# Zero-padded 64-row score matmuls and a later cubic step in a fused attention and GEGLU kernel on one NeuronCore

## The chip, the cores and the metric

The kernel runs on one core of a Trainium2 chip (trn2). The metric is the device time of one execution in microseconds (us). Before the change the median of six runs was 1717.1 us (1713.9 to 1721.9); over all 16 runs of the rounds in which the two kernels were compared it was 1716.66 us.

Engine names in the profile: PE is TensorE's matmul, PEld its weight load, DVE is VectorE, ACT is ScalarE, POOL is GpSimd, SPq is the queue of SyncE from which this kernel issues its loads.

## The reference

A pre-LayerNorm attention block followed by a pre-LayerNorm feed-forward block with a gated GELU, in bfloat16, with S = 2048 rows, width D = 576, 32 heads of 18 columns and F = 4608:

```python
h  = x + A_ref(layernorm(x), wqkv, wo)          # x is A_x; B_x is not used
h2 = h + B_ref(layernorm(h), w_gate, w_up, w_down)
# A_ref: qkv = x @ wqkv; p = softmax(q k^T * 18**-0.5); (p v) @ wo
# B_ref: (gelu_tanh(x @ w_gate) * (x @ w_up)) @ w_down
```

## The kernel before

The queries are cut into 4 blocks of 512 rows, the heads into 8 groups of four. A *unit* is one head group in one block, so there are 32 units (0 to 31). A unit has 32 *passes*. In each pass TensorE computes scores for two heads and 128 keys (two matmuls of 512 columns), and ScalarE turns them into exponentials in one 128 x 1024 instruction. After every second pass TensorE multiplies four heads' exponentials by the values (the PV matmuls).

A head has 18 rows, and a 19th carries a bound that keeps the exponentials in range. So a score matmul has 19 active rows of the 128, placed at one of four 32-row tiles of the array:

```python
KTj = sb("KTj", [P, 2, S], BF16)          # keys of four heads at partitions 0, 32, 64, 96; two units
QTj = sb("QTj", [P, 2, QB], BF16)
a_sb = sb("a_sb", [P, 2, 512], BF16)      # copy of the attention accumulator

def emit_ST(i):                            # the scores of pass i
    ...
    for q_, c in enumerate(cc):            # two of the four heads
        fns.append(mm_fn(Sring[:, bankcol:bankcol + 512],
                         KTj[32 * c:32 * c + PS, s_, kt * P:(kt + 1) * P],        # PS = 19
                         QTj[32 * c:32 * c + PS, s_, :], True, True, tile_position=(32 * c, 0)))
```

All other work is put between the passes as *filler*. Units 0 to 2 carry the Q and K projections. Units 3 to 7 carry nearly nothing. Units 8 to 31 carry the previous block's output projection (Wo), its second LayerNorm and its feed-forward network (FFN). The last block's FFN runs alone after the last exponential; it is called the tail here. Fillers that cost TensorE time draw on a credit of 560 per pass (the scheduler's own unit, meant as ns). The FFN has 36 *f tiles* of 128 columns per block, in two halves of 18. Each half ends with five down projections.

```python
def ffn_gelu_a(f, tail=False):
    ...                                                                    # x2 = xb^2
    if tail: E("act",  lambda e: e.activation(x2, xb, ACTF.Square), ...)
    else:    E("pool", lambda e: e.tensor_tensor(x2, xb, xb, ALU.mult), ...)
    E("dve", lambda e: e.scalar_tensor_tensor(out=x2, in0=x2, scalar=GC1, in1=xb, op0=ALU.mult, op1=ALU.mult), ...)
    E("pool" if tail else "dve", lambda e: e.tensor_tensor(x2, x2, xb, ALU.add), ...)

def ffn_gelu_c(f):
    ...                                                                    # after tanh on ScalarE
    E("dve", lambda e: e.scalar_tensor_tensor(out=x2, in0=th, scalar=1.0, in1=xb, op0=ALU.add, op1=ALU.mult), ...)
    E("pool", lambda e: e.tensor_tensor(gT[:, fs, :], x2, ub, ALU.mult), ...)

# schedule_ffn, for each f tile; at(pass, cost, what)
    if fs == 0:
        ...ffn_load_wd for the first two down-projection tiles...
    if f % FCH == 0 and fc + 1 < NFC:
        ...ffn_load_chunk: gate and up weights of the next two f tiles...
    at(s0, 1100.0, gate)        # 5 matmuls, then the gate is copied out of PSUM (xb)
    at(s0 + 1, 1100.0, up)      # 5 matmuls, then half of the up part is copied out (ub)
    at(s0 + 2, 0.0, ffn_gelu_a)
    at(s0 + 7, 0.0, ffn_gelu_b) # tanh, ScalarE
    at(s0 + 8, 0.0, ffn_gelu_c)
    step[0] += 2                # so s0 advances by two passes per f tile
```

## Time and profile before

| Stage, from the first exponential of one unit to that of the next (the tail: from the end of the last exponential) | us |
|---|---|
| prologue (first LayerNorm, K and V projections) | 114.5 |
| units 0 to 2 (Q/K projections as filler) | 161.9 |
| units 3 to 7 (attention alone) | 152.6 |
| units 8, 16, 24 (Wo and second LayerNorm) | 120.1 |
| unit 9 (the first FFN starts) | 62.1 |
| the other twenty units (FFN as filler) | 902.3 |
| tail | 206.5 |

In the page of the profile, part 1 gives busy time, share of the span and instructions of each engine. In part 2 each digit is the share of one fortieth of the span in tenths; `PEclk` is the clock that TensorE was granted.

```profile
PE 1399.6 (81%) x7528; PEld 458.1 (27%) x7528; DVE 734.3 (43%) x1568; ACT 1126.0 (65%) x1293; POOL 387.6 (23%) x364
...
PEclk9778756555659898998788889696987998869998
```

No engine is full, and the clock stands at 5 to 7 tenths in 15 of the 40 slices. The stretches show where. Columns: from:to and length in us, busy us of each engine (with its instructions), granted clock, DMA share, GB/s.

```profile
114.50:276.40 161.90, 138.09 (x619) 49.11 (x619) 92.22 (x129) 92.02 (x97) 2.30 (x2) 0.74 0.02 8
276.40:429.00 152.60, 140.08 (x667) 27.96 (x667) 11.76 (x36) 150.19 (x162) 5.75 (x5) 0.51 0.04 13
...
469.00:1513.80 1044.80, 890.92 (x4992) 280.55 (x4992) 436.01 (x901) 765.39 (x844) 266.03 (x246) 0.84 0.22 58
1513.80:1720.20 206.40, 148.13 (x708) 61.60 (x708) 109.23 (x209) 62.84 (x108) 97.75 (x76) 0.89 0.32 78
...
278.40:455.80 177.40, 164.09 (x824) 37.99 (x823) 19.04 (x63) 168.72 (x180) 6.46 (x7) 0.50 0.04 14
```

In the second stretch ScalarE is busy 150.19 of 152.60 us: attention alone is bound by the exponentials, 30.5 us per unit. The units with the FFN as filler take 34.5 to 62 us instead, while ScalarE is at 73% there. The last line is the odd one: TensorE is busy 164.09 of 177.40 us, 92%, and its clock is half (0.50) throughout.

The clock records of this trace hold only 0.5 and 1.0, and the stretches of each are multiples of 3.41 us (the last one, at the end of the trace, aside); those at 0.5 add up to 686 us, 40% of the span. Being busy alone is not what decides here: a TensorE that is 92% busy stays slow.

The timeline (start in us, length, engine, line, operation; in brackets the idle time before the instruction and what ended it) shows the second loss. This is the FFN as filler, with the two copies out of PSUM left out:

```profile
914.89 0.69 DVE L724 SCALAR_TENSOR_TENSOR arena<-arena 128x512 bf16<-128x512 bf16 x1 [2.26 <-POOL arena L723]
915.61 0.42 DVE L726 TENSOR_TENSOR arena<-arena 128x512 bf16<-128x512 bf16 x1
...
917.15 0.68 DVE L742 SCALAR_TENSOR_TENSOR arena<-arena 128x512 bf16<-128x512 bf16 x1
917.91 1.15 POOL L744 TENSOR_TENSOR arena<-arena 128x512 bf16<-128x512 bf16 x1 [3.06 <-DVE arena L742]
919.02 1.04 POOL L723 TENSOR_TENSOR arena<-arena 128x512 bf16<-128x512 bf16 x1
920.10 0.69 DVE L724 SCALAR_TENSOR_TENSOR arena<-arena 128x512 bf16<-128x512 bf16 x1 [2.26 <-POOL arena L723]
```

L724 is the cubic step, L742 the (1 + tanh) step, L744 GpSimd's product and L723 its square. The cubic step of one tile is queued on VectorE right behind the square of the same tile, so VectorE waits. The square is queued on GpSimd behind the product of an earlier tile, which waits for VectorE's L742. VectorE and GpSimd take turns in a ring of 5.21 us per f tile, in which neither is full.

The view of waits (engine, tile and line that waited, what it waited for: us in total, times, longest) gives the sums:

```profile
DVE arena L724 <- POOL arena L723: 203.6, 90, 2.3
PE Sring L297 <- ACT PT L576: 84.7, 150, 7.1
PE Aacc L297 <- DVE a_sb L596: 33.2, 12, 4.3
PE G L296 <- DMA arena<-in_B_w_up_dram: 24.4, 10, 5.2
PE G L296 <- POOL arena L744: 17.3, 2, 8.7
```

The first line is the ring. The last is the tail: both halves' down projections wait 8.7 us for GpSimd's last products.

### The profile page before, as it was taken

How to read it: one execution, taken by the hardware profiler on the slowest of the kernel's cores; microseconds unless marked ns; L12 is line 12 of the kernel's file. 1: busy time of each engine (PE TensorE's matmuls, PEld its weight loads, DVE VectorE, ACT ScalarE, POOL GpSimd, SP SyncE). 2: the span in 40 equal slices, each digit the busy share in tenths (PEclk: the TensorE clock that was granted, in tenths of full speed). 3: DMA queues.
4: the chain of work that ended last, by engine and by line, in shares of the span. 5: the costliest groups of instructions: out<-in, count | busy, mean ns of one | idle time of the engine just before them, and what ended most of it. 6: DMA issues, size and time to landing. Idle time of an engine off the chain costs nothing.

```text
span 1720.2 us, 20569 instructions
## 1 busy us (share of the span) xinstructions
PE 1399.6 (81%) x7528; PEld 458.1 (27%) x7528; DVE 734.3 (43%) x1568; ACT 1126.0 (65%) x1293; POOL 387.6 (23%) x364
## 2 busy tenths in 40 slices
PE   2557899999978798878898887888997987968686
PEld 1223222111312232222322222223322322232222
DVE  6546543000435514531555135414553255156364
ACT  3123668999748676778787667677875786725151
POOL 1100000000014402330133114300342134007373
PEclk9778756555659898998788889696987998869998
DMA  3010000000032122211221132022221320123432
GB/s 103 14 40 6 10 10 10 12 17 10 10 92 65 37 58 75 65 34 55 70 69 50 40 89 65 23 56 69 64 60 41 80 70 24 35 69 108 89 86 49
DMA packets 193174, 87.23 MB, mean 51 GB/s; under 512 B 97968, under 2 KB 190064, under 8 KB 193072
## 3 DMA queue, kind: packets, MB, share of 16 engines
q1 hardware_dynamic: 193072, 85.91, 18.8%
q8 instruction: 59, 0.97, 0.2%
q14 instruction: 43, 0.35, 0.1%
HBM read 71.07 MB, written 2.36 MB: 43 GB/s over the span
## 4 chain that ended last, share of the span: by engine, by line
PE 37%; DVE 18%; POOL 14%; issue 14%; ACT 9%; SPq 4%; DMA 4%; POOLq 0%; ACTq 0%; DVEq 0%
PE G L296 21%; PE Sring L297 10%; ACT PT L576 9%; POOL arena L744 7%; PE Aacc L297 4%; POOL arena L723 4%; SPq L288 4%; DVE arena L724 3%; DVE arena L742 3%; DVE arena L322 2%; POOL arena L726 2%; DMA arena<-in_B_w_down_dram 2%; DVE arena L726 2%; PE G L309 1%; DMA arena<-in_B_w_up_dram 1%
## 5 line engine op out<-in xcount | busy, mean ns | idle before, releaser
L576 ACT ACTIVATE PT<-Sring 128x1024 bf16<-128x1024 f32 x1024 | 987.0, 1024 | 347.3 <-PE Sring L297 341.1
L297 PE MATMUL Sring<-QTj,KTj 19*128 19x512 bf16 x2048 | 457.9, 466 | 100.3 <-ACT PT L576 84.7
L296 PE MATMUL G<-hnT,arena 128*128 128x512 bf16 x1440 | 402.3, 418 | 63.6 <-DMA arena<-in_B_w_up_dram 24.4
L296 PE MATMUL G<-arena 128*128 128x512 bf16 (+3 forms) x1120 | 305.8, 426 | 34.9 <-POOL arena L744 17.3
L297 PE MATMUL Aacc<-PT,Vpj 128*32 128x512 bf16 x2048 | 247.5, 473 | 33.9 <-DVE a_sb L596 33.2
L744 POOL TENSOR_TENSOR arena<-arena 128x512 bf16<-128x512 bf16 x144 | 183.4, 1278 | 373.4 <-DVE arena L742 373.4
L297 PEld LDWEIGHTS Sring<-QTj,KTj 19*128 19x128 bf16 x2048 | 95.3, 94 | 475.4 <-ACT PT L576 268.3
L296 PEld LDWEIGHTS G<-hnT,arena 128*128 128x128 bf16 x1440 | 127.9, 104 | 273.1 <-issue 84.0
L724 DVE SCALAR_TENSOR_TENSOR arena<-arena 128x512 bf16<-128x512 bf16 x144 | 110.6, 768 | 203.6 <-POOL arena L723 203.6
L296 PEld LDWEIGHTS G<-arena 128*128 128x128 bf16 (+3 forms) x1120 | 118.8, 119 | 183.8 <-issue 85.0
L552 POOL COPY Vpj<-Vd 128x1152 bf16<-128x1152 bf16 x32 | 36.6, 1146 | 515.5 <-PE Aacc L297 502.1
L723 POOL TENSOR_TENSOR arena<-arena 128x512 bf16<-128x512 bf16 x108 | 112.2, 1039 | 130.3 <-DVE arena L322 130.3
L324 DVE TENSOR_SCALAR arena<-G 128x512 bf16<-128x512 f32 x144 | 98.7, 686 | 95.5 <-PE G L296 63.4
L742 DVE SCALAR_TENSOR_TENSOR arena<-arena 128x512 bf16<-128x512 bf16 x144 | 114.6, 804 | 0.3
L733 ACT ACTIVATE arena<-arena 128x512 bf16<-128x512 bf16 x144 | 89.8, 628 | 31.7 <-DVE arena L726 25.5
L297 PEld LDWEIGHTS Aacc<-PT,Vpj 128*32 128x32 bf16 x2048 | 54.5, 96 | 190.5 <-issue 188.4
L322 DVE CAST arena<-G 128x512 bf16<-128x512 f32 x108 | 74.0, 685 | 50.0 <-PE G L296 50.0
L596 DVE CAST a_sb<-Aacc 128x512 bf16<-128x512 f32 x32 | 22.0, 687 | 170.0 <-PE Aacc L297 170.0
L317 ACT ACTIVATE arena<-G 128x512 bf16<-128x512 f32 x36 | 21.5, 597 | 94.2 <-PE G L296 66.0
L393 POOL TENSOR_TENSOR lnt<-lnt,halfc 128x1 f32<-128x1 f32 x32 | 17.5, 548 | 245.0 <-DVE lnt L392 245.0
L771 DVE COPY arena<-G 128x512 f32<-128x512 f32 (+1 forms) x20 | 13.8, 688 | 106.7 <-PE G L296 106.7
L726 POOL TENSOR_TENSOR arena<-arena 128x512 bf16<-128x512 bf16 x36 | 42.2, 1173 | 41.0 <-DVE arena L724 41.0
(77 smaller groups left out, 558.8 us busy)
## 6 DMA issues: line engine op xcount, KB each, us to landing
arena<-in_B_w_gate_dram SPq DMA_DIRECT2D x72, 256.0 KB, 2.7
arena<-in_B_w_up_dram SPq DMA_DIRECT2D x72, 256.0 KB, 3.2
arena<-in_B_w_down_dram SPq DMA_DIRECT2D x32, 576.0 KB, 4.6
KTj<-KTd SPq DMA_DIRECT2D x128, 76.0 KB
QTj<-QTd SPq DMA_DIRECT2D x128, 19.0 KB
arena<-in_A_x_dram SPq DMA_DIRECT2D x4, 576.0 KB, 4.0
h_sb<-in_A_x_dram SPq DMA_DIRECT2D x4, 576.0 KB, 5.7
arena<-in_B_w_gate_dram SPq DMA_DIRECT2D x72, 32.0 KB, 2.7
```

Source lines behind the costliest of these rows:

```text
L288: fns = [(lambda o, i: lambda e: e.dma_start(o, i))(o, i) for (o, i) in pairs]
L296: return lambda e: e.matmul(dst, lhsT, rhs, start=start, stop=stop)
L297: return lambda e: e.matmul(dst, lhsT, rhs, start=start, stop=stop, tile_position=tile_position, skip_group_check=skip)
L322: E("dve", lambda e: e.tensor_copy(dst_ap, src_ap), reads=reads, writes=writes)
L324: E("dve", lambda e: e.tensor_scalar(dst_ap, src_ap, scale, None, ALU.mult), reads=reads, writes=writes)
L576: E("act", lambda e: e.activation(PT[:, pts, :], Sring[:, slot * 1024:(slot + 1) * 1024], ACTF.Exp, scale=SCALE), reads=[("S", slot * 2), ...
L723: E("pool", lambda e: e.tensor_tensor(x2, xb, xb, ALU.mult), reads=[("xb", k)], writes=[("x2", k)])
L724: E("dve", lambda e: e.scalar_tensor_tensor(out=x2, in0=x2, scalar=GC1, in1=xb, op0=ALU.mult, op1=ALU.mult), reads=[("x2", k), ("xb", k)], ...
L726: E("pool" if tail else "dve", lambda e: e.tensor_tensor(x2, x2, xb, ALU.add), reads=[("x2", k), ("xb", k)], writes=[("x2", k)])
L733: E("act", lambda e: e.activation(th, uu, ACTF.Tanh, scale=GC0), reads=[("x2", k)], writes=[("th", k)])
L742: E("dve", lambda e: e.scalar_tensor_tensor(out=x2, in0=th, scalar=1.0, in1=xb, op0=ALU.add, op1=ALU.mult), reads=[("th", k), ("xb", k)], ...
L744: E("pool", lambda e: e.tensor_tensor(gT[:, fs, :], x2, ub, ALU.mult), reads=[("ub", k), ("x2", k)], writes=[("gT", fs)])
```

## The change

The change has two aims: to get TensorE its full clock by making each score matmul cover 64 rows of the array, of which 45 are zeros, and to open the ring by moving the cubic step two passes later. Several smaller moves come with it. The core of the diff:

```diff
-    KTj = sb("KTj", [P, 2, S], BF16)
-    QTj = sb("QTj", [P, 2, QB], BF16)
+    KTj = sb("KTj", [P, 2, 2, S], BF16)
+    QTj = sb("QTj", [P, 2, 2, QB], BF16)
-    a_sb = sb("a_sb", [P, 2, 512], BF16)
+    a_sb = sb("a_sb", [P, 1, 512], BF16)
 ...                                                      # prologue
+        E("dve", (lambda s_: lambda e: e.memset(KTj[:, s_], 0.0))(s_), writes=[("KTj", s_)])
+        E("dve", (lambda s_: lambda e: e.memset(QTj[:, s_], 0.0))(s_), writes=[("QTj", s_)])
 ...                                                      # loads, each head's 19 rows
-            pairs.append((KTj[32 * c:32 * c + PS, s_, :], KTd[r0:r0 + PS, j, :]))
+            p0 = 64 * (c // 2)
+            pairs.append((KTj[p0:p0 + PS, s_, c % 2, :], KTd[r0:r0 + PS, j, :]))
 ...                                                      # emit_ST
-                             KTj[32 * c:32 * c + PS, s_, kt * P:(kt + 1) * P],
-                             QTj[32 * c:32 * c + PS, s_, :], True, True, tile_position=(32 * c, 0)))
+                             KTj[p0:p0 + 64, s_, c % 2, kt * P:(kt + 1) * P],
+                             QTj[p0:p0 + 64, s_, c % 2, 0:qb], True, True, tile_position=(p0, 0)))
 ...                                                      # ffn_up, tail only: up part copied out by ScalarE
-        evac(ub, bank[:, 0:512], [bkey], [("ub", k)], "dve", scale=0.5)
+                    evac(tmp[:, 1, k, 0:qb], bank[:, 0:qb], [bkey], [("ub", k)], "act" if tail else "dve", scale=0.5)
 ...                                                      # gelu: the cubic step and the add become ffn_gelu_a2
-        E("pool" if tail else "dve", lambda e: e.tensor_tensor(x2, x2, xb, ALU.add),
+        E("dve", lambda e: e.tensor_tensor(x2, x2, xb, ALU.add),
 ...                                                      # schedule_ffn
-                if fs == 0:
-                    ...ffn_load_wd...
-                if f % FCH == 0 and fc + 1 < NFC:
-                    ...ffn_load_chunk...
+                if f % FCH == 0 and fc + 1 < NFC:
+                    ...ffn_load_chunk...
+                if fs == 2:
+                    ...ffn_load_wd...
-                at(s0 + 2, 0.0, (lambda f: lambda: ffn_gelu_a(f, tail=tl))(f))
+                at(s0 + 2, 0.0, (lambda f: lambda: ffn_gelu_a(b, f, tail=tl))(f))
+                at(s0 + 4, 0.0, (lambda f: lambda: ffn_gelu_a2(b, f, tail=tl))(f))
 ...                                                      # Wo: three parts; the second PSUM bank is taken only at the third
-            add_bulk(base + 8 + 2 * qt, 1100.0, (lambda qt: lambda: block_Wo_qt_b(b, qt))(qt), tag)
+            add_bulk(base + 8 + 2 * lt, 900.0, (lambda lt: lambda: block_Wo_qt_b(b, lt))(lt), tag)
+            add_bulk(base + 8 + 2 * lt, 450.0, (lambda lt: lambda: block_Wo_qt_c(b, lt))(lt), tag)
```

Cut here: a table of block sizes (all remain 512 rows), hooks for the FFN's bank and phase that do nothing, a rewritten main loop, the queuing of all three parts of a down projection at one pass, and the many lines that follow from these.

The single `a_sb` buffer is what makes room.

## The prediction

> **What bounds the kernel now.** The table by stretches: prologue (0 to 114 us), attention with Q/K projections as fillers (to 276), attention alone (to 429), attention with three blocks' Wo, LN2 and FFN (to 1514), the last block's FFN alone (206 us). Attention alone runs at 30.1 us per unit (32 units, 8 head groups x 4 blocks) with ScalarE 100% busy on exponentials; 32 units at that pace would be 963 us, but they take 1399. Three causes show.

> 1. A ring of VectorE and GpSimd. In the timeline at 915 to 926 us the FFN repeats every 5.2 us per f tile: VectorE 2.95 us of work, then idle 2.26 us (203.6 us in the waits view) for GpSimd's product (1.15) and square (1.04), because the cubic step directly follows the square. Eight tiles per unit are 42 us, which is what the full-clock units 10 and 29 take. ScalarE needs 4 x 0.94 + 0.63 = 4.4 us per tile. The same blocking delays the copy of the attention accumulator (33 us of PE waits, up to 4.3 each) and, at each half's end, the tanh ahead of the exponentials (6.5 us stalls).
> 2. The clock: half rate for 40% of the time, in multiples of 3.41 us.[...] At 278 to 456 us TensorE is 92% busy and yet at half rate. Weighting matmuls by active rows x columns (scores 19/128, PV 1/4), a window under about 0.38 of full-rate work is followed by a slow one, in all but some 10 of 490 windows. A slow window costs 1.1 to 2 us (equal units 20 and 28: 43.0 and 39.6 us with 3 and 1).
> 3. In the tail GpSimd does 2.7 us per f tile; tiles pass every 3.3 us, and the down matmuls wait 8.7 us twice.

> **What the change does.**
> - Scores become 64-row tiles padded with zeros: same streaming time[...], weight 1/2 instead of 0.15. Applied to the old windows, slow ones fall from 24 to about 6 in units 0 to 2 and from 97 to about 45 from unit 9 on. Attention alone (0.33 to 0.38) mostly stays slow, at no cost.
> - The cubic step moves two steps later: the ring opens, toward 4.4 to 4.7 us per tile.
> - Tail: the add leaves GpSimd for VectorE, the up eviction goes to ScalarE (4 x 0.61 = 2.45 us per tile, the new bound).
> - Weight-load order, Wo split, single a_sb buffer: about nothing.
> - Added: zeroing KTj and QTj on VectorE before the first LN, estimated 4.5 us from the 1.48 us for 1710 words, critical.

> **Sum.** Prologue +4.5; units 0 to 2 -17; 3 to 7 -2; 8, 16, 24 -9; unit 9 -10; the other twenty from 45 to about 39 us: -125; tail -30. 1717 - 188 is about 1530 us; range 1470 to 1620. Faster by over 2%: 0.95; within: 0.035; slower: 0.015.

> **Right or wrong shows as:** VectorE's wait for the square under 40 us; mean clock about 0.85 to 0.9; gate/up units at 37 to 40 us; attention-alone units still 30; tail near 175 us, ScalarE its busiest elementwise engine; first LN about 4.5 us later.

> **Wrong if:** padding zeros don't count as activity (then about 1590); exponentials and fillers couple so that units stay above 41 us; weight loads bind the tail.

The terms come to -188.5 us, and 1717 - 188 is about 1530. What it says of the hardware stands beside these numbers: a pair of score matmuls takes 0.39 us at full clock and 0.61 at half in both profiled runs ("same streaming time"); 0.94 us is a unit of 30.1 us over its 32 exponentials; the "1.48 us for 1710 words" is VectorE's zeroing of 128 x 1710 words at 1.23 us of before. Estimates from the windows of before are the 0.38, the counts of slow windows that padding would leave, the 0.33 to 0.38 of attention alone, and the cost of a slow window (units 20 and 28 by themselves give (43.0 - 39.6) / 2 = 1.7 us).

## More of the kernel before

All loads go through one queue, SyncE's. That includes the copies of the next unit's keys and queries, which `jit_loads` issues at pass 8 of each unit as eight loads in a row (four of KTj, four of QTj).

## The result, and the profile after

The kernel after takes 1554.57 us, the median of 8 runs (1552.1 to 1557.0), against 1716.66 us. The ratio is 0.9055, with a 95% interval of 0.9035 to 0.9075. Ratios here are the mean time of one kernel's fast runs over that of the other's of the same rounds, so they are not quite the ratio of the medians quoted. Outputs were correct, as in all the runs below. The profiled runs span 1720.2 and 1552.7 us.

The same two parts of the page, for the kernel after:

```profile
PE 1276.3 (82%) x7528; PEld 442.7 (29%) x7528; DVE 824.9 (53%) x1572; ACT 1131.6 (73%) x1329; POOL 393.5 (25%) x328
...
PEclk9878899565689999999899999998999999969998
```

TensorE runs the same 7528 matmuls in 123 us less busy time, as the clock rose from 0.801 to 0.888 on average. Mainly the attention-alone part remains slow (0.61). The stretches of the kernel after, cut at the same units:

```profile
119.50:262.30 142.80, 115.17 (x620) 44.54 (x619) 92.04 (x129) 91.02 (x96) 2.30 (x2) 0.92 0.03 9
262.30:412.50 150.20, 128.44 (x667) 27.33 (x667) 11.67 (x36) 149.32 (x161) 5.75 (x5) 0.61 0.04 14
...
443.80:1365.00 921.20, 816.99 (x5005) 271.06 (x5004) 520.11 (x918) 758.05 (x844) 315.23 (x247) 0.94 0.25 66
1365.00:1552.70 187.70, 142.21 (x708) 64.96 (x708) 115.26 (x209) 78.28 (x144) 54.94 (x40) 0.88 0.35 86
```

The waits of the kernel after:

```profile
PE Sring L308 <- ACT PT L637: 89.6, 176, 5.7
PE G L307 <- DMA arena<-in_B_w_up_dram: 45.8, 16, 5.5
PE G L307 <- POOL arena L846: 15.5, 2, 7.7
DVE arena L824 <- ACT arena L815: 10.2, 4, 5.4
```

VectorE's 203.6 us for GpSimd's square are gone; of the cubic step's waits (now L824) 10.2 us for the tail's square on ScalarE are left. TensorE's 33.2 us of waits for the copy of the attention accumulator, which VectorE makes, are gone too (they are back, at 36.1 us, when experiment 4 closes the ring again). TensorE's waits for up weights rose from 24.4 to 45.8 us. The timeline of the FFN as filler, one f tile:

```profile
842.35 0.69 DVE L844 SCALAR_TENSOR_TENSOR arena<-arena 128x512 bf16<-128x512 bf16 x1
842.96 0.68 DVE L824 SCALAR_TENSOR_TENSOR arena<-arena 128x512 bf16<-128x512 bf16 x1
843.12 1.53 POOL L846 TENSOR_TENSOR arena<-arena 128x512 bf16<-128x512 bf16 x1 [1.66 <-DVE arena L844]
843.68 1.26 DVE L826 TENSOR_TENSOR arena<-arena 128x512 bf16<-128x512 bf16 x1
...
846.30 0.68 DVE L844 SCALAR_TENSOR_TENSOR arena<-arena 128x512 bf16<-128x512 bf16 x1
```

The period is now 3.95 us (842.35 to 846.30), no longer 5.21. The add (L826) takes 1.26 us where it took 0.42. It now runs beside GpSimd's product, L846, which is itself slower (1.53 against 1.15 us). In this trace 128 of VectorE's 144 adds run beside a product and take 1.25 or 1.26 us each; the other 16, beside no product, take 0.42. The products beside an add take 1.47 to 1.54 us. The mean of the adds went from 425 ns (108 of them; the tail's were GpSimd's then) to 1166 ns (all 144). Why the two slow each other when they run side by side, called their collision below, no run here shows. It costs VectorE time; what it costs of the total is taken up below.

Set against the prediction, stage by stage (the sum by stage of the profiled runs):

| Stage | before | after | change predicted | change measured |
|---|---|---|---|---|
| prologue | 114.5 | 119.5 | +4.5 | +5.0 |
| units 0 to 2 | 161.9 | 142.8 | -17 | -19.1 |
| units 3 to 7 | 152.6 | 150.2 | -2 | -2.4 |
| units 8, 16, 24 | 120.1 | 94.0 | -9 | -26.1 |
| unit 9 | 62.1 | 51.1 | -10 | -11.0 |
| other twenty units | 902.3 | 807.2 | -125 | -95.1 |
| tail | 206.5 | 187.8 | -30 | -18.7 |
| **total** | 1720.2 | 1552.7 | -188 | -167.5 |

So 30 us are missing in the twenty FFN units and 11 in the tail, while the Wo units gained 17 more than predicted. The experiments look for these, and for whether the two causes are really the two that were named.

### The profile page after: what moved, and what is told of

Its sections match the earlier page's. It is cut to its first block, busy times and chain, and to the rows that moved or that the text cites. A ratio compares the mean times of both kernels' runs of the same rounds, so it can differ in the third digit from the quotient of the medians.

```text
span 1552.7 us, 20513 instructions
## 1 busy us (share of the span) xinstructions
PE 1276.3 (82%) x7528; PEld 442.7 (29%) x7528; DVE 824.9 (53%) x1572; ACT 1131.6 (73%) x1329; POOL 393.5 (25%) x328
## 5 line engine op out<-in xcount | busy, mean ns | idle before, releaser
L308 PE MATMUL Sring<-QTj,KTj 64*128 64x512 bf16 x2048 | 428.7, 427 | 106.9 <-ACT PT L637 89.6
L307 PE MATMUL G<-hnT,arena 128*128 128x512 bf16 x1440 | 366.0, 394 | 46.6 <-DMA arena<-in_B_w_up_dram 45.8
L307 PE MATMUL G<-arena 128*128 128x512 bf16 (+3 forms) x1120 | 281.5, 401 | 29.8 <-POOL arena L846 15.5
L846 POOL TENSOR_TENSOR arena<-arena 128x512 bf16<-128x512 bf16 x144 | 213.8, 1485 | 305.1 <-DVE arena L844 282.0
L308 PE MATMUL Aacc<-PT,Vpj 128*32 128x512 bf16 x2048 | 225.6, 430 | 0.7 <-ACT PT L637 0.7
L308 PEld LDWEIGHTS Sring<-QTj,KTj 64*128 64x128 bf16 x2048 | 97.1, 94 | 436.6 <-ACT PT L637 257.7
L826 DVE TENSOR_TENSOR arena<-arena 128x512 bf16<-128x512 bf16 x144 | 167.8, 1166 | 5.0
L307 PEld LDWEIGHTS G<-arena 128*128 128x128 bf16 (+3 forms) x1120 | 112.6, 114 | 167.1 <-issue 62.2
L844 DVE SCALAR_TENSOR_TENSOR arena<-arena 128x512 bf16<-128x512 bf16 x144 | 118.1, 820 | 12.3 <-ACT arena L834 11.4
L342 DVE TENSOR_SCALAR arena<-G 128x512 bf16<-128x512 f32 x108 | 74.0, 685 | 62.4 <-PE G L307 62.0
L824 DVE SCALAR_TENSOR_TENSOR arena<-arena 128x512 bf16<-128x512 bf16 x144 | 98.2, 682 | 10.2 <-ACT arena L815 10.2
```

Of the source, the lines that this page charges most:

```text
L307: return lambda e: e.matmul(dst, lhsT, rhs, start=start, stop=stop)
L308: return lambda e: e.matmul(dst, lhsT, rhs, start=start, stop=stop, tile_position=tile_position, skip_group_check=skip)
L342: E("dve", lambda e: e.tensor_scalar(dst_ap, src_ap, scale, None, ALU.mult), reads=reads, writes=writes)
L826: E("dve", lambda e: e.tensor_tensor(x2, x2, xb, ALU.add), reads=[("x2", k), ("xb", k)], writes=[("x2", k)])
L846: E("pool", lambda e: e.tensor_tensor(gT[:, fs, 0:qb], x2, ub, ALU.mult), reads=[("ub", k), ("x2", k)], writes=[("gT", fs)])
```

## The experiments

Theory A: TensorE's clock depends on how much of its array is at work, zeros included, and the opened ring gives the rest; the missing 30 us are a new wait. Rival theories: B, the padding does nothing by itself (or the clock follows the speed of the pipeline, not the rows), and the later cubic step gives all; C, the reverse; D, the small moves have effects of their own, against the prediction's "about nothing".

Each part of the change was made alone or undone alone. In what follows "before" and "after" are the two kernels. The twelve runs came in three calls; the median of before in their rounds was 1720.28, 1719.26 and 1718.93 us. For the four runs of the second call (experiments 5 to 8) the record's own verdict against before is "unclear": before ran from 1694 to 1726 us there. What is read of these four is the median against that of after, and the stages; their own runs lie within 0.6% of each other.

### 1. The padding alone

Before, with the padded operands, the zeroing, and the single `a_sb` that it needs:

```diff
-    KTj = sb("KTj", [P, 2, S], BF16)            # QTj alike
+    KTj = sb("KTj", [P, 2, 2, S], BF16)
-                             KTj[32 * c:32 * c + PS, s_, ...], ... tile_position=(32 * c, 0)
+                             KTj[64 * (c // 2):64 * (c // 2) + 64, s_, c % 2, ...], ... tile_position=(64 * (c // 2), 0)
```

> The kernel before plus the padding alone (64-row score tiles, zeroed KTj and QTj, single a_sb for room). Clock theory (the throttle counts active rows, padded zeros too): prologue +5 us, units 0 to 2 about -19, units 8, 16, 24 about -26 together, unit 9 about -10, the other filled units about -50 through fewer slow windows, tail unchanged at 206; total about 1615 us, mean clock about 0.87. Rival (padding is only a layout; the clock rose because the stalls went away): 1717 to 1725 us, clock stays 0.80.

Measured: 1659.88 us, ratio 0.9655 (0.961 to 0.970), clock 0.873. Units 0 to 2 fell from 161.9 to 142.9 us, all that they gain in after. So B falls: zeros in the array raise the clock (0.801 in before). But the total fell by 60 us, not by the 105 expected: the other twenty units gained 34 of 50 us, units 8, 16 and 24 12 of 26, unit 9 4 of 10, and the prologue cost 7. In the FFN units the ring of VectorE and GpSimd still stands (its wait is 203.6 us here too), which limits what a faster TensorE can gain there. The clock of this kernel by fortieths of the span, to compare with the two above:

```profile
PEclk9768898555779899999899999998999998969898
```

### 2. The later cubic step alone

Before, with the cubic step and the add moved to `s0 + 4`:

```diff
+    def ffn_gelu_a2(f, tail=False):
 ...
+                at(s0 + 4, 0.0, (lambda f: lambda: ffn_gelu_a2(f, tail=tl))(f))
```

> The kernel before plus the later cubic step alone. Ring theory: VectorE's wait for the square falls from 204 us to under 40, the full-clock gate/up stretches go from 5.2 to about 4.4 us per f tile, total about 1650 us; units 0 to 2 stay at 162 us and 8, 16, 24 at 120 us because their clock is unchanged. Rival (the stalls are what slows the clock, padding does nothing): about 1560 us and clock near 0.88.

Measured: four runs from 1659.25 to 1689.12 us, two of which count as slow (over 1.5% above the fastest). The two fast ones give a ratio of 0.9692 (0.962 to 0.977), about 53 us. The profile fell in the slow state, so only what the ring's opening cannot blur is read from it: VectorE's wait for the square is gone, and units 0 to 2 still take 158 us and units 8, 16 and 24 still 120. Both causes count, and neither gives the whole, so C falls too.

### 3. After, with 19 rows again

Everything of the change except the padding: operands, loads and score matmuls as before; the zeroing is kept at its cost.

```diff
-                             KTj[p0:p0 + 64, s_, c % 2, kt * P:(kt + 1) * P], ... tile_position=(p0, 0)
+                             KTj[32 * c:32 * c + PS, s_, kt * P:(kt + 1) * P], ... tile_position=(32 * c, 0)
```

> The changed kernel with the scores back at 19 rows in 32-row tiles (zeroing kept, so the prologue stays at 119 us). Clock theory: units 0 to 2 back to about 161 us, 8, 16, 24 back to about 120, some 30 us more in the FFN units; about 1630 us, clock about 0.82. Rival (layout only): 1550 to 1560 us, clock 0.89.

Measured: 1617.39 us, ratio 0.9403 (0.936 to 0.945), clock 0.812. The padding is worth 63 us in after, as it was worth 60 in before. The stretch of units 0 to 2 of this kernel has the length and the clock that it had in before, to the digit:

```profile
119.00:280.90 161.90, 138.07 (x619) 49.04 (x619) 92.18 (x129) 91.98 (x97) 2.30 (x2) 0.74 0.02 8
```

### 4. After, with the cubic step at once

```diff
-                at(s0 + 4, 0.0, (lambda f: lambda: ffn_gelu_a2(b, f, tail=tl))(f))
+                at(s0 + 2, 0.0, (lambda f: lambda: ffn_gelu_a2(b, f, tail=tl))(f))
```

> The changed kernel with the cubic step back directly behind the square. Ring theory: VectorE waits for the square again by some 150 us or more, f tiles at 5.2 us in the gate/up stretches (108 x 0.9 = about +95), but the 4.4 us stalls for the up weights go away in exchange (about -40); about 1605 us. The product's slow-down of the add (1.26 us when it overlaps GpSimd) disappears: the add is 0.43 us again. Rival (VectorE is not what paces these units): within 1% of 1555 us.

Measured: 1610.89 us, ratio 0.9373 (0.934 to 0.941), clock 0.885. The clock is that of after (0.888), so the two causes are separate. The waits of this kernel show the ring back in full, and the wait for up weights small again:

```profile
DVE arena L824 <- POOL arena L817: 203.6, 90, 2.3
PE G L307 <- DMA arena<-in_B_w_up_dram: 18.1, 8, 5.4
```

The second line is the first hint at the missing 30 us: the wait for up weights is 18.1 us with the ring closed and 45.8 with it open (closed: 24.4 in before and 27.9 with the padding alone; open: 44.8 in experiment 3). The add takes 500 ns on the mean here, 1166 in after.

### 5. After, with 32 rows

The layout of experiment 3, but the matmul covers 32 rows (19 and 13 zeros):

```diff
-                             KTj[32 * c:32 * c + PS, s_, ...]
+                             KTj[32 * c:32 * c + 32, s_, ...]
```

> The changed kernel with scores in four 32-row tiles as before, but all 32 rows active (13 of them zeros). If the throttle counts active rows x columns, a score matmul weighs 32/128 = 0.25, between 0.148 (19 rows) and 0.5 (64 rows): applied to the windows of the 19-row variant, slow ones fall from 178 to about 160, so about 1590 us, clock about 0.83, and 0.25 should be the weight that sorts its windows best. If the throttle counts whole row groups, or only data that isn't zero, nothing changes against 19 rows: 1617 us, clock 0.81.

| Kernel (rows of a score matmul) | windows | 0.148 (19 rows) | 0.25 (32) | 0.5 (64) |
|---|---|---|---|---|
| before (19) | 491 | **0** | 19 | 76 |
| after with 19 rows | 459 | **1** | 21 | 69 |
| after with 32 rows | 451 | 10 | **0** | 38 |
| padding alone (64) | 471 | 41 | 26 | **1** |
| after (64) | 441 | 40 | 27 | **1** |

(These counts take a matmul to stream from 0.08 us after its recorded start, an offset that was fitted; without it the bold counts are 5, 4, 3, 3 and 3. The limit is sharp: at 0.36 the bold counts are 7 to 19, at 0.39 they are 7 to 12. Six more kernels, on which nothing was fitted, give 0 to 4 misses of 426 to 481 windows.)

In each kernel the weight that fits is the number of rows that the instruction covers, whether they hold data or zeros. The 92% busy stretch at half clock fits: with scores of 19 rows its 50 windows sum to 0.15 to 0.34, none to 0.375. Attention alone stays mostly slow even when padded (0.61; 7 of the 43 windows in that stretch of after reach 0.375). But there ScalarE is busy 149.32 of 150.20 us and TensorE 128.44, so the exponentials bind, and the slow clock costs nothing that shows: 30.04 us per unit, against 30.5 in before.

### 6. After, with the tail's engines as before

```diff
-                    evac(... "act" if tail else "dve", scale=0.5)
+                    evac(... "dve", scale=0.5)
-        E("dve", lambda e: e.tensor_tensor(x2, x2, xb, ALU.add),
+        E("pool" if tail else "dve", lambda e: e.tensor_tensor(x2, x2, xb, ALU.add),
```

> The changed kernel with the last block's add back on GpSimd and its up eviction back on VectorE. My reading: the tail goes back from 188 to about 205 us, everything before it unchanged; about 1572 us. Rival (the tail's gain comes from the later cubic step or the load order): tail about 190, 1555 us.

Measured: 1576.34 us, ratio 0.9205 (0.913 to 0.929), the tail at 208 us. Without these two moves nothing of the tail's gain is left (206.5 us in before), and it is some 20 us, not the 30 of the prediction.

### 7. After, with the down-projection weights loaded first

```diff
+                if fs == 0:
+                    ...ffn_load_wd...
                 if f % FCH == 0 and fc + 1 < NFC:
                     ...ffn_load_chunk...
-                if fs == 2:
-                    ...ffn_load_wd...
```

> The changed kernel with the two w_down loads issued at a half's first tile and ahead of the next w_gate/w_up chunk, as before. If this order is what took units 12, 20 and 28 from about 42 to 36 us and unit 9 down by some 8: about +28 us, 1582 us, with TensorE waiting for the up weights right after a half's start. If the order costs nothing (as I predicted): 1555 us, and the cause is elsewhere in the rest of the change.

Measured: 1569.35 us, ratio 0.9168 (0.909 to 0.925). This order is worth 15 us, about half of the 28 expected here, and the prediction had put it at nothing (D holds). The cost sits where a half of the FFN starts: unit 9 takes 60.7 us (51.1 in after), unit 12 42.0 (36.1). In the waits of this kernel the up weights stand at 57.9 us:

```profile
PE G L307 <- DMA arena<-in_B_w_up_dram: 57.9, 21, 6.6
```

### 8. After, with Wo in two parts and two banks

```diff
-            add_bulk(base + 8 + 2 * lt, 900.0, ...block_Wo_qt_b...)
-            add_bulk(base + 8 + 2 * lt, 450.0, ...block_Wo_qt_c...)
+            add_bulk(base + 8 + 2 * lt, 1100.0, ...block_Wo_qt_b...)   # _a takes both banks, as before
```

> The changed kernel with Wo back in two pieces that hold two of the three banks. If the split is what took units 8, 16 and 24 from 36 us each (padding alone) to 31: about +13 us there, 1567 us. If it is worth nothing (as I predicted): 1555 us.

Measured: 1561.14 us (1558.5 to 1567.0), ratio 0.9123 (0.902 to 0.923). By itself the total does not settle it, for the interval holds after's 0.9055. The stage does: units 8, 16 and 24 take 109.0 us instead of 94.0. Part of these 15 us comes back in unit 9 and in units 17 and 25, which get less left-over work. Whether it is the credit (2000 against 2250 per row tile) or the bank held early was not separated. What shows: in unit 8, which is 4.7 us longer than in after, TensorE waits 3.6 us for VectorE's adds and copies that follow the Wo matmuls, against 0.6 in after.

### 9. After, with the first down projection spread into the end of a half

At a half's end TensorE's scores waited up to 5.7 us behind ScalarE (first line of after's waits). The three parts of the first down projection were set 7, 5 and 2 passes earlier, to give TensorE work while the last tiles pass through the elementwise engines:

```diff
-                    at(s0, n_mm * 220.0, fn)
+                    at(s0 - (7, 5, 2)[ip] if m == 0 else s0, n_mm * 220.0, fn)
```

> The changed kernel with the first down tile's three parts issued between the last cubic/tanh chains of a half instead of after all of them. If the missing gain in the units with a half's end is the exponentials queued behind the last tanhs (stalls of 5.7 and 5.1 us, six of them, each followed by slow windows): stalls under 2 us, about 1530 us, units 11, 14, 19, 22, 27, 30 from 44 to about 39 us, tail unchanged at 188. If those stalls are paid for elsewhere anyway: within 1% of 1555.

Measured: 1546.42 us, ratio 0.9017 (0.896 to 0.908): 8 us, a third of the 25 expected; the units with a half's end fell from 43.8 to 42.3 us, not to 39. The long waits for the exponentials went, as the waits of this kernel show, but TensorE now waits at other places, for GpSimd's last products:

```profile
PE Sring L308 <- ACT PT L637: 63.4, 180, 0.7
PE G L307 <- POOL arena L846: 40.0, 8, 7.7
```

The stall moved rather than went away.

### 10. After, with the loads of keys and queries spread

Why did the units that carry only gate and up matmuls (10, 13, 18, 21, 26, 29) stay at 42 us, when the ring was open? The load queue of after shows eight key and query loads issued in a row, and the weights behind them. Here the second column is how long the queue was taken by the group:

```profile
811.82 2.58 SPq L299 DMA_DIRECT2D KTj<-KTd  x4
814.45 7.98 SPq L299 DMA_DIRECT2D QTj<-QTd  x4
822.53 3.48 SPq L299 DMA_DIRECT2D arena<-in_B_w_gate_dram  x2
826.37 1.85 SPq L299 DMA_DIRECT2D arena<-in_B_w_up_dram  x2
```

The keys and queries hold the queue for 10.6 us, and the next weights' issue begins only then. TensorE's timeline in the same unit of after shows the price: it idles 4.38 us for the up weights, and the five matmuls that follow take 2.10 us (1.25 us in the group before): its clock record, at 1.0 during the stall, is at 0.5 from 832.70 to 836.11 us.

```profile
832.43 2.10 PE L307 MATMUL G<-hnT,arena 128*128 128x512 bf16 x5 [4.38 <-DMA arena<-in_B_w_up_dram]
```

The experiment issues one head's keys and queries at each of passes 2, 8, 14 and 20, the same eight loads in all:

```diff
-        if p == min(8, blk(b)[4] - 1) and u + 1 < NU:
-            jit_loads(u + 1)
+        if p in (2, 8, 14, 20) and u + 1 < NU:
+            jit_loads(u + 1, heads=((p - 2) // 6,), copy=(p == 8))
```

> The changed kernel with the next unit's K and Q loads issued head by head over the unit instead of all eight at once. If the 4.4 us stalls for the up weights in units 10, 13, 18, 21, 26, 29 come from weight loads standing behind some 10 us of K and Q issue on the one load queue: these stalls go, those units fall from 42 to about 36 us, about 1520 us. If the weights are late for another reason (bandwidth, two slots only): stalls stay, 1555 us.

Measured: 1506.47 us, ratio 0.8792 (0.873 to 0.885), so 48 us faster than after, more than the 35 expected. The six units fell from 42 to 35.3 us each. Each load now holds the queue about 0.6 us:

```profile
800.38 0.64 SPq L299 DMA_DIRECT2D KTj<-KTd  x1
801.07 0.60 SPq L299 DMA_DIRECT2D QTj<-QTd  x1
...
806.82 0.96 SPq L299 DMA_DIRECT2D arena<-in_B_w_gate_dram  x2
```

And the wait for up weights in this kernel is

```profile
PE G L307 <- DMA arena<-in_B_w_up_dram: 14.8, 8, 5.4
```

So the missing time of the gate/up units was the load queue. In before the ring of 5.21 us per tile was slow enough to hide most of it. The packet records of the traces tell more of why eight loads in a row take 10.6 us and not eight times 0.6. The four key loads cost the queue no more in a row (2.58 us) than apart (4 x 0.64); the query loads behind them do (7.98 us). Meanwhile the rows of the keys, 76 packets of 4096 bytes, pass in single file: one every 0.155 us for most of the time from 813.3 to 826.8 us, and for every one of the 32 units of after such a group takes 12.5 to 13.7 us. The queries' rows follow only then. In experiment 10 one head's 19 rows take 3 to 4.3 us at a time, while the queue is already free. So the queue is held while the keys' rows drain; why, no run here shows.

### 11. After, with the cubic step one pass later still

```diff
-                at(s0 + 4, 0.0, (lambda f: lambda: ffn_gelu_a2(b, f, tail=tl))(f))
+                at(s0 + 5, 0.0, (lambda f: lambda: ffn_gelu_a2(b, f, tail=tl))(f))
```

> The changed kernel with the cubic step one more step later, so that the add tends not to run beside a GpSimd product. If the add's 1.17 us (0.43 before) is waiting for GpSimd and not a slower instruction: its mean falls to under 0.8 us with the same count and shape. If VectorE does not pace the units now: total within 1% of 1555 us all the same. If it does: 1535 us or less.

Measured: 1563.38 us over six runs, ratio 0.912 (0.907 to 0.917). The add fell to 929 ns only, and the total rose by 9 us (0.6%); scores now waited up to 6.4 us. The total stayed within the 1% expected, but the premise (an add of at most 0.8 us) was not reached. Nor did VectorE get time back: the cubic step rose from 682 to 914 ns, so the add's 34 us less stand against 33 more there, and VectorE is busy 821.5 us against 824.9. The collision moved from one step to the other. So this run says nothing about what the collision costs.

### 12. After with 9, 10 and the zeroing on GpSimd

```diff
-        E("dve", (lambda s_: lambda e: e.memset(KTj[:, s_], 0.0))(s_), writes=[("KTj", s_)])   # and QTj
+        if 1 <= t <= 4:                                          # between the first LayerNorm's row tiles
+            E("pool", (lambda s_, h_: lambda e: e.memset(KTj[:, s_, h_, :], 0.0))((t - 1) // 2, (t - 1) % 2), ...)
+        if 5 <= t <= 6:
+            E("pool", (lambda s_: lambda e: e.memset(QTj[:, s_], 0.0))(t - 5), ...)
```

> The half-end order and the split loads together, and the zeroing of KTj and QTj on GpSimd during the first LN tiles instead of on VectorE ahead of them. If the three costs are separate: prologue back to about 115 us, both kinds of stall gone, about 1555 - 25 - 35 - 5 = 1490 us. If they overlap: 1510 us or more.

Measured: 1504.51 us, ratio 0.8776 (0.871 to 0.885): the fastest of all, but only 2 us below experiment 10, with overlapping intervals, and between the 1490 us expected of separate costs and the 1510 of overlapping ones. The prologue gained nothing (119.4 us). LayerNorm did start at 13.5 us again and not at 18.9, but then its row tiles followed every 5.0 us and not every 3.9, and VectorE's instructions were long where they met GpSimd's zeroing. In the timeline of this kernel:

```profile
27.98 1.80 POOL L541 MEMSET KTj<- 128x2048 bf16 x1
28.53 1.42 DVE L418 TENSOR_SCALAR arena<-arena,lnt 128x576 bf16<-128x576 bf16 x1
```

The same instruction took 0.35 us in before. Here it ended at 28.53 + 1.42 = 29.95, some 0.2 us after the end of the zeroing at 29.78. Why it is long beside the zeroing, no run here shows.

### What the parts add up to

| Part undone in after | median, us | costs |
|---|---|---|
| padding (19 rows) | 1617.39 | 62.8 |
| later cubic step | 1610.89 | 56.3 |
| engines of the tail | 1576.34 | 21.8 |
| order of the weight loads | 1569.35 | 14.8 |
| Wo in three parts | 1561.14 | 6.6 |
| sum | | 162.3 |

The whole change is worth 1716.66 - 1554.57 = 162.1 us, so the parts add up within the noise. Not undone alone were the single `a_sb`, the zeroing and the queuing of a down projection's parts at one pass. The medians are from different rounds. Taken from the ratios instead, the five sum to 171 us, each uncertain by some 5 to 20 us, so the close match of the medians is partly luck.

## Why the prediction was right or wrong

The range and the two main mechanisms, the ring and the clock, held; the estimate of 1530 us was 25 us too low. It was that near in part by luck: 41 us were missing in the twenty units and the tail, but units 8, 16 and 24 gave 17 us more than predicted, most of it from a move that had been put at nothing.

- **The ring: right.** VectorE's wait for the square went from 203.6 us to nothing, and experiment 4 brings it back to the microsecond. Moving the cubic step is worth 53 to 56 us.
- **The clock through padded rows: right, and the riskiest claim.** Clock 0.801 to 0.888 ("about 0.85 to 0.9"). Windows at half clock fell from 25 to 7 in units 0 to 2 (predicted 24 to 6) and from 97 to 35 from unit 9 to the tail (predicted 97 to 45). Three row counts, each with its own weight, confirm that zeros count. For zeros that don't count the prediction had named about 1590 us; with 19 rows again (experiment 3) it is 1617.
- **Prologue, units 0 to 2, attention alone: right** within about 2 us each. The first LayerNorm came 5.4 us later against 4.5.
- **Unit 9: the right number by luck.** It fell by 11.0 us against 10, but the padding alone brings only 3.6 there, experiment 3 without the padding still has 49.9 us, and undoing the load order (experiment 7) takes 9.6 of the 11.0 back. The gain came from a move that was put at nothing.
- **"the other twenty from 45 to about 39 us: -125": the term that was mis-sized.** They fell to 40.4 us, 95 us in all. The step that failed is "gate/up units at 37 to 40 us". They stayed at 42 (44 on the mean in before), for a reason other than before's: the opened ring met the load queue, which eight key and query loads in a row hold for 10.6 us. Experiment 10 changes only that, brings those units to 35.3 us and the kernel to 1506 us. The prediction counted weight loads as a risk of the tail only. The trace of before already had the wait, at 24.4 us. The six units with a half's end stayed at 43.8 us too, so twelve of the twenty are above the 41 us that the prediction had named as a sign of being wrong; in experiment 9 theirs came down to 42.3 only, and what holds them there is open.
- **"Weight-load order, Wo split, single a_sb buffer: about nothing": wrong for the first two.** The load order is worth 15 us (experiment 7), for the same queue's sake. The Wo split is worth 15 us in units 8, 16 and 24 (experiment 8), part of which comes back later. This is where those units' 26 us came from, against the 9 that the clock was to give: the padding alone brings 12.4 (experiment 1), and undoing the Wo split takes 15.0 back. The single `a_sb` was needed for the room; it was not tested alone, and no wait for it of over 1.3 us shows in after.
- **"tail -30", "tail near 175 us, ScalarE its busiest elementwise engine": wrong in size and in the engine.** The steady pace did become 2.50 us per f tile, from 3.27 (time between (1 + tanh) steps in the two timelines), which over 36 tiles is 28 us. But TensorE's waits for up weights in the tail rose from 3.0 to 10.3 us, and the two waits for GpSimd's last products went only from 8.7 to 7.7 us. "weight loads bind the tail" was named as a risk, and a part of it came true. In the tail's stretch VectorE is busy 115 us and ScalarE 78. In the steady part of after's tail VectorE starts its three steps 0.60, 0.71 and 1.18 us apart without a gap, the add taking 1.26 us beside the product, and ScalarE idles 0.38 us per tile. The prediction did not count the collision. It cost little against its own figure, though: 2.50 instead of 2.45 us per tile.

So where a size was off, the cause is mostly one: the prediction took away two limits and did not ask what the next limit of each stage would be.

Still open: why the queue is held while the keys' rows drain, what exactly in the Wo split helps, what keeps the units with a half's end at 42 to 44 us, and what the collision of VectorE's steps with the product costs in total.

## What to carry to other kernels

When TensorE runs small matmuls and its granted clock is low although it is busy (here 0.50 at 92%), weigh each matmul by the share of the array that it covers. In these traces the next window was slow where the weighted work came to less than 0.375, and more rows of zeros were worth 60 us (experiment 1) and 63 us (experiment 3), at the cost of room and of zeroing them once (5.0 us of prologue in after).

When an engine waits for its partner in front of other work, as VectorE did for 203.6 us here, move the waiting step later in its queue by at least the partner's whole turn. Then look at once for what the old wait was hiding: here a queue that held weight loads behind eight small loads, which cost 48 us more.

Small moves in the order of issue deserve their own estimate. Two that looked like nothing were worth 15 us each, one in the total and one in its stage.
